# Plain records and interleaved channel pairs in the S4 tables of a fused S4 + MLP training kernel

## The chip, the cores and the metric

The kernel runs on one NeuronCore of a Trainium2 chip. A core has a matrix engine (TensorE, "PE" in the profile, with its weight loads as "PEld"), a vector engine (VectorE, "DVE"), a scalar engine (ScalarE, "ACT"), GpSimd ("POOL") and SyncE ("SP"), which here only starts transfers; 16 DMA engines move the data. The five instruction streams run side by side and meet through semaphores. The metric is the device time of one launch in microseconds.

## What is computed

Sequence length L = 2048, D = 448 channels, N = 256 complex states per channel, MLP width F = 1792, all bf16. The output is a gated sum of a long convolution (the S4 branch `a`) and a two-layer MLP with squared ReLU (`b`); the kernel returns it and 14 gradients.

```python
g  = sigmoid((u * gate_w).sum(-1))
# S4: K[d,l] = Re sum_n C*dt*B*exp(dt*A)^l ; a = irfft(rfft(u) * rfft(K)) + u*Dskip
P  = exp(logdA[:, :, None] * arange(L))
K  = einsum("dn,dnl,dn->dl", Cc, P, dB).real
# MLP
r  = relu(u @ w1 + b1);  b = (r * r) @ w2 + b2
out = g * a + (1 - g) * b
_out, _vjp = jax.vjp(f, A_u, ..., gate_w); grads = _vjp(grad_out)
```

The powers P = lambda^l are never formed for all l. With l = 48 b + s, a table X holds 16 small powers times the weight W = C·dt·B (`Xs`) and a table Y the giant steps (`Ys`); K is the product X·Y, one matmul for each channel and pair of table halves. The gradient of C, B and A needs the transposed sums with dK, the gradient of K.

## The kernel before

**Up to 248 us.** Everything to line 663 is put in order by the compiler's scheduler: loads and a first transform of u and of the gradient (the FFT is done as matmuls; `fwd1`, `fwd2`, `inv1`), and beside them `powers` (L573 to L590): 12 squarings of lambda for four groups of up to four chunks of 32 channels. Each level is copied by ScalarE from float32 into the group's record (L577, into strided fields), squared by ScalarE (L586) and combined by VectorE (L587, L588); the finished records go to DRAM (`rec_d`, L590). The product of the spectra (`cmul`, L274 to L279) and `inv1` end in `hd` in DRAM, which is loaded again (L302); the matmuls of L637 make dK, which goes through DRAM (`dk_d`, L648) back into the tile `DK` (four DMAs, L653 and L654).

**The loop, about 248 to 640 us.** From `tc.manual_schedule()` (L1002) the order of every instruction stream is the order in which the code is written. The loop runs over 14 chunks of 32 channels, and for each chunk over the tokens of one string. The "D" tokens are steps of the MLP (first layer, projection, then the second layer's backward pass), 13 in a chunk, 127 in all:

```python
PERIOD = """XS YS LR D X0 Z0 D SA X1 Z1 D X2 D Z2 D Y0 Y1 SV D T0 Y2 D P0 D S0 Z3 FX0 Y3 D FX1 T1 Y4 KM KO D P1 D FY0 S1 D FY1 FY2 D"""
```

The tokens X, Y, XS, YS, KM and KO work on chunk c, the tokens T, Z, P and S on chunk c-1:

- LR loads the next chunk's record (L718, GpSimd's queue); FX and FY let ScalarE spread it into full-width multipliers (L726 to L737); XS and YS (L713, L741) copy the seeds.
- X0 to X2 double the table X by one product (L683) and one sum (L684) each; Y0 to Y4 do so for Y (L697, L700, sums L706). All VectorE.
- KM (L770) is 128 small TensorE matmuls X·Y into the PSUM tile psX, KO (L777) copies them out, and then starts four DMA transposes of Y (L796, SP's queue), one for each group g of 8 channels.
- SA (four ScalarE copies, L802) and SV (one VectorE product, L806) put dK and 16·b·dK of the chunk into matmul operands `DKc`.
- Z0 to Z3 multiply group g's transposed Y with these (L821, PSUM tile psF) and copy out (ScalarE, L823). T0 and T1 transpose half of X on TensorE, 16 transposes into the same PSUM tile psF (L790). P0 and P1 are two VectorE products of the two (L833, L834), S0 and S1 sum them over 16 entries with a selection matrix (L850).
- A first-layer step is 8 matmuls (L911, L914), two ReLUs on ScalarE (L918) and a square on VectorE two steps later (L921); a second-layer step is 8 matmuls (L973, L976), two scalings (L978) and a VectorE product (L981). A projection half-step is 7 matmuls (L894). The second layer first loads its operand from `DBT_d` in DRAM (L957), which the program starts shortly before.

**Behind the loop.** The last chunk's Z, T, P and S, a reload of K, its transform, another `cmul`, the remaining weight gradients of the MLP as filling work (L1104 to L1123), `param_grads` (L1292 to L1342, a VectorE generator called for four groups of channels) and the outputs.

Of the kernel before, what the change touches and what calls it, by code (L numbers as in the profile page):

```python
# [316 lines left out]
def kernel(ctx, tc, A_u, A_A_re, A_A_im, A_B_re, A_B_im, A_C_re, A_C_im, A_log_dt, A_Dskip,  # L317
# [95 lines left out]
    vw_np = np.array([[slot_offsets().get(i % 64, 0) + 16 * (b if i % 64 < 40 else 0) for b in range(NA)] for i in range(128)], np.float32).astype(ml_dtypes.bfloat16)  # L413
    vw = const.tile([P, NA], bf16, name="vw")
    nc.sync.dma_start(vw[:], nc.inline_tensor(vw_np, name="cs_vw").ap())
# [123 lines left out]
    psets = [(Fp[:, 0:4 * RS], RA[:, 14336:16384], W0[:, 3584:4608]), (RA[:, 0:4 * RS], RA[:, 8704:10752], SB[:, 10240:11264])]  # L539

    def fields(r):

        xs = r[:, :, 0:512].rearrange("p c (t w r e) -> p c t w r e", t=2, r=2, e=2)
        ys = r[:, :, 512:1024].rearrange("p c (w t e) -> p c t w e", t=2, e=4)
        lx = r[:, :, 1024:1408].rearrange("p c (t l w) -> p c t w l", t=2, w=W2)
        ly = r[:, :, 1408:2176].rearrange("p c (t l w) -> p c t w l", t=2, w=W2)
        return xs, ys, lx, ly
    for rb, _, _ in psets:
        xs, ys, _, _ = fields(rb.rearrange("p (c r) -> p c r", c=4))
        for t in range(2):  # L550
            G_.memset(xs[:, :, t, :, 0, 0], 1.0 - t)
            G_.memset(ys[:, :, t, :, 0], 1.0 - t)
            G_.memset(ys[:, :, t, :, 3], 0.0)

# [3 lines left out]
    def powers(gr):  # L558
        nch = min(4, NCH - 4 * gr)
        cs_ = slice(4 * gr, 4 * gr + nch)  # L560
        n = nch * W2
# [11 lines left out]
        S.copy(xs[:, :, :, :, 1, 0], Wt[:, cs_])  # L573
        x, y = Lam[:, :, cs_], halves(cur[0])
        for k in range(NLEV):
            dst = ys[..., 1] if k == 3 else ys[..., 2] if k == 11 else xs[..., 0, 1] if k == 4 else lx[..., LEVX[k]] if k in LEVX else ly[..., LEVY[k]]
            S.copy(dst.rearrange("p c t w -> p t c w"), x)  # L577
# [73 lines left out]
    for cpy in range(2):  # L651
        qe = nc.scalar if cpy else G_
        qe.dma_start(DK[64 * cpy:64 * cpy + 40], bass.AP(tensor=dk_d, offset=0, ap=[[16 * D, 40], [D, 16], [1, D]]))  # L653
        qe.dma_start(DK[64 * cpy + 40:64 * cpy + 41, 0], bass.AP(tensor=dk_d, offset=640 * D, ap=[[D, 1], [1, D]]))  # L654


# [21 lines left out]
    X2 = 2 * W2
    def step_x(c, n, k):

        lo = Xs[c % 2][:, 0:1]
# [1 line left out]
        V.tensor_tensor(out=Vt[:, 0:2 * w * n], in0=run(lo, 0, [0, 2], [NA, w], [1, n]), in1=run(PX[:, 0:1], 512 * k, [2, w], [0, n], [1, 2]), op=ALU.mult)  # L683
# [886 lines left out]
```

## Time and profile before

| | us |
|---|---|
| runs | 915.91, 918.64, 899.32; median 915.91 |
| profiled execution, its span | 902.5 |
| VectorE busy | 635.3 (70%) |
| TensorE busy | 625.3 (69%) |
| ScalarE busy | 512.8 (57%) |
| GpSimd busy | 207.0 (23%) |

The span runs from the first to the last instruction of one profiled execution; its own time outside the profile is not recorded, and the three runs lie between 3 us below the span and 16 us above it. No engine is busy throughout, so the shares over the whole span say little: the program has stages with different limits, and each has to be read by itself. In a row of the trace "x" is a count, "L" a line of the kernel, and the arrow in a wait points to the instruction or transfer that ended it.

### The profile page before, as it was taken

Reading aid. Unit: us, or ns where it says so; the run is one execution under the profiler, and the core shown is the slowest. Engines: PE = TensorE matmul, PEld = TensorE weight load, DVE = VectorE, ACT = ScalarE, POOL = GpSimd, SP = SyncE. Lnnn points to the kernel's source line nnn. Section 1 sums busy time; section 2 is a strip of 40 time slices with the busy share of each in tenths; the row PEclk is TensorE's granted clock in tenths of the full one; section 3 lists DMA queues with packets and bytes.
Section 4 is the critical chain, followed back from the end, with each engine's and each line's share of the span. In section 5 each row is a group of like instructions: output and inputs, shape, how many; then the busy total and the mean of one; then the engine's idle time right before and its main releaser. Section 6 shows DMA issues by size and latency. Waiting matters only on the chain. (4 is left out here: it accounts for less than half of the span.)

```text
span 902.5 us, 16581 instructions
## 1 busy us (share of the span) xinstructions
PE 625.3 (69%) x6596; PEld 301.3 (33%) x6621; DVE 635.3 (70%) x1004; ACT 512.8 (57%) x820; POOL 207.0 (23%) x320
## 2 busy tenths in 40 slices
PE   3755454426178887878667777777779787898794
PEld 1212111102024443435423333343545343444341
DVE  4795997761478889987639877978647865765360
ACT  0777877840366646676544655546566577344451
POOL 1253000141111212211232332313125311131121
PEclk9865555556589999999578997999979899989797
DMA  9858675589387795885696999769769999997951
GB/s 187 220 136 314 241 280 202 197 288 257 88 170 143 164 118 149 174 182 96 105 237 154 193 220 154 219 114 248 179 227 310 357 302 294 297 268 255 221 139 32
DMA packets 183583, 183.40 MB, mean 203 GB/s; under 512 B 124790, under 2 KB 159122, under 8 KB 182914
## 3 DMA queue, kind: packets, MB, share of 16 engines
q1 hardware_dynamic: 151596, 88.98, 44.9%
q0 software_dynamic: 22480, 71.68, 26.9%
q10 hardware_dynamic: 9430, 21.69, 6.8%
q8 instruction: 52, 0.85, 0.4%
q14 instruction: 25, 0.20, 0.1%
HBM read 84.76 MB, written 68.91 MB: 170 GB/s over the span
## 5 line engine op out<-in xcount | busy, mean ns | idle before, releaser
L823 ACT CAST P<-psF 128x1024 bf16<-128x1024 f32 x56 | 62.2, 1112 | 53.8 <-PE psF L821 48.0
L683 DVE TENSOR_TENSOR F<-X,F 128x1024 bf16<-128x1024 bf16 (+2 forms) x42 | 64.3, 1531 | 2.1 <-ACT F L729 1.5
L894 PEld LDWEIGHTS <-U 128*128 128x128 bf16 x448 | 41.9, 102 | 45.9 <-issue 16.3
L911 PE MATMUL psN<-S,K 128*128 128x512 bf16 x155 | 43.8, 414 | 16.3 <-ACT S L918 14.2
L973 PE MATMUL psN<-S,K 128*128 128x512 bf16 x156 | 44.0, 410 | 15.1 <-DMA S<-DBT_d 13.2
L1117 PEld LDWEIGHTS <-S 128*128 128x128 bf16 x416 | 40.0, 101 | 39.7 <-issue 12.0
L1117 PE MATMUL psX<-D,S 128*128 128x449 bf16 x224 | 51.5, 377 | 1.6 <-ACT S L1123 0.7
L833 DVE TENSOR_TENSOR M<-P,psF 128x2048 bf16<-128x2048 bf16 x28 | 34.1, 1217 | 25.2 <-PE psF L790 22.9
L821 PE MATMUL psF<-R,S 41*32 41x256 bf16 x896 | 24.6, 291 | 38.8 <-ACT P L823 22.7
L894 PE MATMUL psN<-D,U 128*128 128x448 bf16 x224 | 51.2, 378 | 0.0
L899 POOL DMA_DIRECT2D br_d<-D x32 | 17.7, 553 | 145.0 <-ACT D L898 142.5
L894 PE MATMUL psN<-S,U 128*128 128x448 bf16 x224 | 50.4, 374 | 0.0
L978 ACT ACTIVATE U<-psN 128x512 bf16<-128x512 f32 x56 | 30.5, 611 | 32.6 <-PE psN L976 32.6
L1108 ACT ACTIVATE S<-psN 128x1024 bf16<-128x1024 bf16 x32 | 33.0, 1030 | 19.4 <-PE psN L1104 19.3
L802 ACT COPY S<-K 128x128 bf16<-128x128 bf16 x56 | 34.9, 1024 | 13.5 <-DMA K<-dk_d 13.5
L1117 PE MATMUL psX<-K,S 128*128 128x448 bf16 x192 | 40.9, 357 | 1.5 <-ACT S L1120 1.5
L790 PE MATMUL psF<-ident,X 128*128 128x128 bf16 x448 | 35.8, 244 | 8.7 <-ACT P L823 8.6
L981 DVE TENSOR_TENSOR U<-U,D 128x1024 bf16<-128x1024 bf16 x28 | 18.9, 688 | 30.1 <-ACT U L978 30.1
L790 PEld LDWEIGHTS <-X 128*128 128x128 bf16 x448 | 32.8, 111 | 15.3 <-issue 13.6
L293 PE MATMUL psN<-D,cb_MI 64*128 64x448 bf16 x48 | 20.4, 553 | 23.6 <-DVE D L276 5.5
L684 DVE TENSOR_TENSOR X<-F 128x512 bf16<-128x512 bf16 (+2 forms) x42 | 35.6, 848 | 1.4
L898 ACT CAST D<-psN 128x448 bf16<-128x448 f32 x32 | 17.2, 536 | 33.4 <-PE psN L894 30.8
(334 smaller groups left out, 1643.9 us busy)
## 6 DMA issues: line engine op xcount, KB each, us to landing
sp<-K ACTq DMA_DIRECT2D x8, 896.0 KB
D<-rT_d POOLq DMA_DIRECT2D x28, 256.0 KB, 6.0
dhT_d<-U POOLq DMA_DIRECT2D x28, 256.0 KB, 4.8
R<-sp SPq DMA_DIRECT2D x8, 896.0 KB
S<-dhT_d POOLq DMA_DIRECT2D x14, 512.0 KB, 5.5
R<-hd SPq DMA_DIRECT2D x16, 448.0 KB
rec<-rec_d POOLq DMA_DIRECT2D x12, 544.0 KB, 7.3
S<-rT_d POOLq DMA_DIRECT2D x12, 512.0 KB, 6.9
```

What stands on the lines that cost most here:

```text
L683: V.tensor_tensor(out=Vt[:, 0:2 * w * n], in0=run(lo, 0, [0, 2], [NA, w], [1, n]), in1=run(PX[:, 0:1], 512 * k, [2, w], [0, n], [1, 2]), o ...
L684: V.tensor_tensor(out=run(lo, n, [NA * X2, 2], [NA, X2], [1, n]), in0=run(vb, 0, [n * X2, 2], [n, X2], [1, n]), in1=run(vb, (w + X2) * n, ...
L790: T_.transpose(ps[:, t, 128 * b:128 * b + 128], Xs[c % 2][:, o_:o_ + 128], ident[:])
L802: S.copy(D2[:, :, 0, 4 * l:4 * l + 4].rearrange("p (g i) a -> p a g i", g=NG), DK[:, l::4].rearrange("p a (e g q i) -> p a e q g i", g=NG, ...
L823: S.copy(zbs[c, g // 2][:, :, g % 2].rearrange("p t h k n -> p t k h n"), psz[:].rearrange("p t (k h n) -> p t k h n", k=2, h=2))
L833: V.tensor_tensor(out=pr.rearrange("p t g h k n -> p t (g h k n)"), in0=zv, in1=xv, op=ALU.mult)
L894: T_.matmul(ps[:, 0:D], lhsT=hblk[:, j, P * tt:P * tt + P], rhs=ws[:, j, :], start=(w == 1 and j == 0), stop=(j == FT - 1))
L911: T_.matmul(pss[k][:], lhsT=w1w[:, dt, j * P:j * P + P], rhs=UT[:, dt, 512 * lb:512 * lb + 512], start=(dt == 0), stop=False, skip_group_c ...
L973: T_.matmul(pss[k][:], lhsT=w2Tw[:, jp, dt, k], rhs=dblk[:, dt], start=(dt == 0), stop=False, skip_group_check=True)
L978: S.mul(hblk[:, 2 * jp + k], pss[k][:], 2.0)
L1108: S.activation(hn(i)[:, 8 * th:8 * th + 8, :], ps[:], ACT.Square if i < FT else ACT.Copy)
L1117: T_.matmul(ps[:, 0:w], lhsT=hn(i)[:, t, :], rhs=(DB2[:, t, :] if i < FT else U[:, t, 0:w]), start=(t == 0), stop=(t == LT - 1))
```

## The change

The tables now hold two channels side by side in the innermost position (an element pair is two channels, not two table entries), and everything around them follows:

- **Records.** 14 plain vectors of 128 numbers a chunk (`RS` 1792 instead of 2176), written in three groups of 4, 7 and 3 chunks with one pair of power buffers in place of two sets. They are loaded by two DMAs: 640 seeds, and nine pieces of 256 bytes a partition straight into a double-buffered multiplier tile `PW`; ScalarE then only makes a copy and a negated copy (`expand`, L735 and L736).
- **X and Y.** Each X product is split in two instructions. The seeds take one copy more, and ones are written once ahead of the loop. The last two levels of Y (`split_y`, L713) are four products without a sum, so Y has 57 columns instead of 41; KO adds the halves (three ScalarE copies, one VectorE sum, L775).
- **dK.** `DK` holds every row twice, in the order of Y's 114 rows, and is loaded by 25 DMAs (L651 and the row behind it) instead of 4. `scale_v` makes both operands by two VectorE products (L802); the ScalarE copies `scale_a` are gone.
- **Z, T, P, S.** A Z is 8 matmuls of 114 rows and 512 columns instead of 16 of 41 rows and 256. T transposes only the half of X that is not multiplied by W: 8 transposes a half, into psX instead of psF. The transposes of Y are of quarters (t, channel half) and no longer of groups, so that Z0 and Z1 need two of them, and Z2 and Z3 all four. `param_grads` multiplies by W itself, six VectorE operations more for each of its four groups.
- **Order.** T1 moves from before KM to behind KO and one D; the square of the first layer is done by ScalarE at once (L915).

The core of the diff:

```diff
-PERIOD = """XS YS LR D X0 Z0 D SA X1 Z1 D X2 D Z2 D Y0 Y1 SV D T0 Y2 D P0 D S0 Z3 FX0 Y3 D FX1 T1 Y4 KM KO D P1 D FY0 S1 D FY1 FY2 D"""
+PERIOD = """XS YS LR D X0 Z0 D X1 Z1 D X2 D Z2 D Y0 Y1 SV D T0 Y2 D P0 D S0 Z3 Y3 D Y4 KM KO D T1 FE D P1 D S1 D"""
 def step_x(c, n, k):
-    V.tensor_tensor(out=Vt[:, 0:2 * w * n], in0=run(lo, 0, [0, 2], [NA, w], [1, n]), in1=run(PX[:, 0:1], 512 * k, [2, w], [0, n], [1, 2]), op=ALU.mult)
+    for r in range(2):
+        V.tensor_tensor(out=run(vb, 128 * n * r, [256 * n, 2], [1, 128 * n]), in0=run(lo, 2048 * r, [0, 2], [32, 64], [1, 2 * n]), in1=factor(c, k, 0, 128, n), op=ALU.mult)
...
+def split_y(c, l, dst, *src):
+    for v in range(2):
+        o_ = run(yb, 2 * dst, [128, 64], [1, 16]) if v == 0 else run(yb, 4096 + 2 * dst + 32, [-4096, 2], [128, 32], [1, 16])
+        V.tensor_tensor(out=o_, in0=run(yb, 0, [128, 64], *src), in1=factor(c, 3 + l, v, 64, 8), op=ALU.mult)
...
+    q.dma_start(PW[c % 2].rearrange("p (l k) -> p l k", k=256)[:, :, 64:192], bass.AP(tensor=rec_d, offset=c * P * RS + 640, ap=[[RS, P], [128, 9], [1, 128]]))
+def expand(c):
+    S.copy(v[:, :, 0], v[:, :, 1])
+    S.mul(v[:, :, 3], v[:, :, 2], -1.0)
 def k_out(c, ps):
-    S.copy(KS[:, :, cp % 4, cc], ps[:].rearrange("p i s -> p s i"))
+    S.copy(ko[:, :, 0:24], ps[:, :, 0:24])
+    S.copy(ko[:, :, 40:41], ps[:, :, 24:25])
+    S.copy(kt, ps[:, :, 41:57])
+    V.tensor_tensor(out=ko[:, :, 24:40], in0=ps[:, :, 25:41], in1=kt, op=ALU.add)
 def scale_v(c):
-    V.tensor_tensor(out=D2[:, :, 1], in0=D2[:, :, 0], in1=run(vw[:, 0:1], 0, [0, CC], [1, NA]), op=ALU.mult)
+    for s_ in range(2):
+        V.tensor_tensor(out=run(DKc[c % 2][:, 0:1], 512 * s_, [2, NA], [32, NA], [1, 2]), in0=dk, in1=run(vw[0:NR, 0:1], 0 if s_ else 2 * NA, [2 if s_ else 0, NA], [0, NA], [1, 2]), op=ALU.mult)
 def back_z(c, g):
+    for s_ in range(2):
+        for k in range(4):
+            T_.matmul(psz[32 * k:32 * k + 32, s_], lhsT=DKc[c % 2][:, 512 * s_ + 128 * g + 32 * k:512 * s_ + 128 * g + 32 * k + 32], rhs=run(YT[0:NR, 0:1], 128 * (8 * g + k), [4096, 2], [512, 2], [1, P]),
...
-                    YTs[c] = [load_yt(c, g) for g in range(NG)]
+                    for j in (0, 2, 1, 3):
+                        load_yt(c, j)
...
+GRP = ((0, 4, Fp), (4, 11, RA), (11, 14, Fp))
-        if q < 2:
-            powers(q + 2)
+        if q == 0:
+            powers(2)
+    for p0, n, r0 in ((0, 24, 0), (50, 16, 24), (82, 16, 24)):
+        for w in range(2):
+            for k in range(4):
+                (nc.scalar if w else nc.sync).dma_start(DK[p0 + w:p0 + 2 * n:2, 4 * k:4 * k + 4], ...)
...
-                later(sq)
+                S.activation(hblk[:, 2 * jp:2 * jp + 2].rearrange("p k l -> p (k l)"), r, ACT.Square)
...
+        mul(x1, Wr, Tr); mul(x2, Wi, Ti); mul(acc, Wr, Ti); sub(WTr, x1, x2)
+        mul(x1, Wi, Tr); stt(nWTi, acc, -1.0, x1, ALU.subtract)
```

Three places show how it moves instructions. First, VectorE at the end of the loop's second chunk, before: the two Y2 products and their sum, P0 (L833, L834; M and P are its tiles), the four products and the sum of Y3 and Y4, P1, and the next chunk's seeds (R and Y are the two Y tables, F the temporary).

```order
L697 TENSOR_TENSOR F_192_1468<-R_188_1460,F_192_1468 128x256x8 x2
L706 TENSOR_TENSOR R_188_1460<-F_192_1468 128x128x16
L833 TENSOR_TENSOR M_193_1469<-P_191_1463,psF_1844 128x2048
L834 TENSOR_TENSOR P_191_1463<-P_191_1463,psF_1844 128x2048
L700 TENSOR_TENSOR F_192_1468<-R_188_1460,F_192_1468 128x128x8 x4
L706 TENSOR_TENSOR R_188_1460<-F_192_1468 128x128x16
L833 TENSOR_TENSOR M_193_1469<-P_191_1463,psF_1924 128x2048
L834 TENSOR_TENSOR P_191_1463<-P_191_1463,psF_1924 128x2048
```

The same place after the change; L828 and L829 are P, L713 is `split_y`, L775 the new sum of KO, which reads the result of KM from psX.

```order
L828 TENSOR_TENSOR M_194_1433<-P_191_1420,psX_1780 128x2048
L829 TENSOR_TENSOR P_191_1420<-P_191_1420,psX_1780 128x2048
L713 TENSOR_TENSOR R_188_1417<-R_188_1417,F_192_1431 128x64x16
L713 TENSOR_TENSOR R_188_1417<-R_188_1417,F_192_1431 128x2x32x16
L713 TENSOR_TENSOR R_188_1417<-R_188_1417,F_192_1431 128x64x16
L713 TENSOR_TENSOR R_188_1417<-R_188_1417,F_192_1431 128x2x32x16
L775 TENSOR_TENSOR P_191_1420<-psX_1843,S_8_163 128x8x16
L828 TENSOR_TENSOR M_194_1433<-P_191_1420,psX_1989 128x2048
L829 TENSOR_TENSOR P_191_1420<-P_191_1420,psX_1989 128x2048
```

The sum of Y4 is gone from VectorE's stream, and between Y4 and P1 stands an instruction that needs KM's result and ScalarE's copy of it. Second, TensorE in the chunk in which the second layer's first step comes (L973 before, L966 after). Before, the end of T1 (L790) and the beginning of KM (L770):

```order
L790 MATMUL psF_4494<-ident,X_190_1462 128x128
L790 LDWEIGHTS X_190_1462
L790 MATMUL psF_4494<-ident,X_190_1462 128x128
L770 LDWEIGHTS X_190_1462
L770 MATMUL psX_4514<-R_188_1460,X_190_1462 32x41
L770 LDWEIGHTS X_190_1462
```

After the change, in the same chunk, the end of the second layer's step that now follows KM directly (L969 is its 64-row part), and T1 (L789):

```order
L969 MATMUL psN_338_4267<-S_8_163,K_180_1253 128x512
L969 LDWEIGHTS K_180_1253
L969 MATMUL psN_339_4268<-S_8_163,K_180_1253 128x512
L789 LDWEIGHTS X_190_1419
L789 MATMUL psX_4279<-ident,X_190_1419 128x128
L789 LDWEIGHTS X_190_1419
```

T1 stood ahead of KM and stands behind KM and a whole D step now, in this chunk behind the step that waits for `DBT_d`; in the others behind a first-layer step, half a projection or a second-layer step. Third, SP's queue of transfers ahead of the loop, after the change (D and P take `hd`, the first K rows the weights w1, the next K rows dK):

```order
L729 DMA rec_1432<-rec_d 128x640
L380 DMA M_178_1242<-c_Ew 128x3712
L311 DMA D_89_656<-hd 64x4x896 x4
L311 DMA P_179_1244<-hd 64x4x896 x4
L730 DMA F_192_1431<-rec_d 128x9x128
L998 DMA K_180_1253<-in_B_w_dram 128x3x1792
L1000 DMA K_180_1253<-in_B_w_dram 64x1792 x2
L651 DMA K_180_1253<-dk_d 24x4x448 x4
L651 DMA K_180_1253<-dk_d 16x4x448 x8
```

Before, SP held no load of dK (two on ScalarE's queue and two on GpSimd's), and the weights w1 stood ahead of the loads of `hd`.

More of the change, by code (lines that the diff above doesn't have):

```diff
@@ L33 @@
 NLEV = 12
-RS = 2176
+RS = 1792
+RC = 2176
 NA = 16
@@ L37 @@
 NY = 41
+NP = 57
 LAG = 2
@@ L412 @@
     make_identity(nc, ident[:])
[L413 to L415 removed]
+    vw_np = np.zeros((P, NA + 1, 2), np.float32)
+    for i in range(2 * NP):
+        p = table_position(i // 2)
+        for b in range(NA):
+            vw_np[i, b, i % 2] = slot_offsets()[p] + 16 * (b if p < 40 else 0)
+        vw_np[i, NA, i % 2] = 1.0
+    vw = const.tile([P, 2 * NA + 2], bf16, name="vw")
+    nc.sync.dma_start(vw[:], nc.inline_tensor(vw_np.reshape(P, -1).astype(ml_dtypes.bfloat16), name="cs_vw").ap())
     dsk_bc = const.tile([P, D], bf16, name="dsk_bc")
@@ L538 @@
     Fp = K.t("F17", [P, 8704])
[L539 to L553, printed above, removed]
+    GRP = ((0, 4, Fp), (4, 11, RA), (11, 14, Fp))
+    cur = [RA[:, 12544 + 1792 * i:14336 + 1792 * i].bitcast(fp32) for i in range(2)]
+    sqr = W0[:, 3584:5376].bitcast(fp32)
     LEVY = {2: 0, 8: 1, 0: 2, 10: 3, 9: 4, 1: 5}
@@ L650, with run @@
                 q.dma_start(bass.AP(tensor=dk_d, offset=128 * e * D, ap=[[D, 16], [16 * D, 8], [1, D]] if e < 5 else [[D, 1], [1, D]]), st_)
[L651 to L654, printed above, removed]
+    for p0, n, r0 in ((0, 24, 0), (50, 16, 24), (82, 16, 24)):
+        for w in range(2):
+            for k in range(4):
+                (nc.scalar if w else nc.sync).dma_start(DK[p0 + w:p0 + 2 * n:2, 4 * k:4 * k + 4], bass.AP(tensor=dk_d, offset=(16 * r0 + k) * D, ap=[[16 * D, n], [4 * D, 4], [1, D]]))
+    nc.scalar.dma_start(DK[48:50, 0], bass.AP(tensor=dk_d, offset=640 * D, ap=[[0, 2], [1, D]]))
+    def run(base, off, *dims):
+        return bass.AP(tensor=base.tensor, offset=base.offset + off, ap=[list(base.ap[0])] + [list(d) for d in dims])
     RB = K.t("R32", [P, 16384])
@@ L678, with factor @@
-    X2 = 2 * W2
+    Pr = [P2[:, 2048 * i:2048 * i + 2048].rearrange("p (s t g n) -> p s t g n", s=2, t=2, g=2) for i in range(2)]
+    vb = Vt[:, 0:1]
+    def factor(c, lv, v, pairs, n):
+        return run(PW[c % 2][:, 0:1], 256 * lv + 128 * v, [2, pairs], [0, n], [1, 2])
     def step_x(c, n, k):
         lo = Xs[c % 2][:, 0:1]
-        w = 2 * X2
-        V.tensor_tensor(out=Vt[:, 0:2 * w * n], in0=run(lo, 0, [0, 2], [NA, w], [1, n]), in1=run(PX[:, 0:1], 512 * k, [2, w], [0, n], [1, 2]), op=ALU.mult)
-        V.tensor_tensor(out=run(lo, n, [NA * X2, 2], [NA, X2], [1, n]), in0=run(vb, 0, [n * X2, 2], [n, X2], [1, n]), in1=run(vb, (w + X2) * n, [-n * X2, 2], [n, X2], [1, n]), op=ALU.add)
@@ L835, in back_p, with back_s @@
+        V.tensor_tensor(out=pr.rearrange("p s t g n -> p s (t g n)"), in0=zv, in1=run(xb, 0, [0, 2], [1, 1024]), op=ALU.mult)
+        V.tensor_tensor(out=z4, in0=z4, in1=run(xb, 512, [0, 2], [-512, 2], [1, 512]), op=ALU.mult)
         return pr, zb
-    def back_s(c, Q, h):
+    def back_s(c, Q, hf):
         nonlocal sps
         cc = c % GC
-        gs = (2 * h, 2 * h + 1)
-        if cc == 0 and h == 0:
+        if cc == 0 and hf == 0:
             sps = K.ps("S", [P, 2, 256])
         for t in range(2):
-            for k in range(2):
-                off = 24 - 16 * cc - 8 * k
-                for gg, g in enumerate(gs):
+            for s_ in range(2):
+                off = 17 - s_ - 16 * cc
+                for gg in range(2):
@@ L1038, in token @@
                 load_rec(c + 1)
-        elif o[0:2] in ("SA", "SV"):
+        elif o == "SV":
             if new:
-                (scale_a if o == "SA" else scale_v)(c)
+                scale_v(c)
         elif o[0] == "X":
```

232 lines of the change are left out of this document (99 added, 133 removed).

## The prediction

> **What bounds the kernel now.** I read the page's first part, then the trace by stages, then the waits of the loop, then one chunk row by row. The page says that no engine is full:
>
> ```profile
> PE 625.3 (69%) x6596; PEld 301.3 (33%) x6621; DVE 635.3 (70%) x1004; ACT 512.8 (57%) x820; POOL 207.0 (23%) x320
> ```
>
> The busy times by stretch (start and end, length, busy of PE, PEld, DVE, ACT, POOL, granted clock, DMA share, GB/s) show where VectorE carries the time:
>
> ```profile
> 187.00:248.10 61.10, 19.18 (x258) 7.59 (x261) 21.56 (x29) 14.87 (x25) 13.92 (x14) 0.58 0.74 205
> 248.10:420.20 172.10, 140.82 (x2015) 69.67 (x2020) 147.09 (x177) 109.80 (x164) 32.66 (x52) 0.92 0.76 148
> 420.20:463.40 43.20, 24.25 (x356) 14.07 (x355) 22.77 (x28) 20.42 (x27) 10.15 (x16) 0.60 0.86 158
> 463.40:640.00 176.60, 134.92 (x1968) 67.75 (x1978) 148.12 (x178) 100.41 (x158) 52.71 (x81) 0.91 0.90 187
> ```
>
> The second row is six chunks beside first-layer steps: 28.7 us each, VectorE 24.5, TensorE 23.5. The fourth is six chunks beside the second layer: 29.4, 24.7, 22.5. So VectorE is idle for only 4.2 and 4.7 us a chunk; its work and its waits together are a chunk's length, and TensorE is 5 to 7 us behind. The third row is the change of layers, a chunk stretched by a wait. The main waits of the loop (who waited, for whom: total, times, longest):
>
> ```profile
> PE psF L821 <- ACT P L823: 21.6, 16, 3.5
> DVE U L981 <- ACT U L978: 26.9, 7, 16.3
> DVE M L833 <- PE psF L790: 19.1, 11, 4.3
> PE psN L973 <- DMA S<-DBT_d: 13.2, 1, 13.2
> PE psF L821 <- DMA R<-R: 10.0, 7, 3.7
> ```
>
> VectorE's own two are P waiting for T (19.1, or 1.5 a chunk) and the second layer's product waiting for ScalarE (26.9, of which 16.3 at the change of layers, so 1.8 a chunk in the second half). TensorE loses 1.7 a chunk to ScalarE's copies of Z and little to the transposes.
>
> **VectorE's work in a chunk.** Durations by form (busy, mean ns):
>
> ```profile
> L706 DVE TENSOR_TENSOR R<-F 128x2048 bf16<-128x2048 bf16 x12 | 14.7, 1225 | 0.4
> L700 DVE TENSOR_TENSOR F<-R,F 128x1024 bf16<-128x1024 bf16 x24 | 15.2, 684 | 0.0
> L683 DVE TENSOR_TENSOR F<-X,F 128x1024 bf16<-128x1024 bf16 x12 | 13.0, 1081 | 0.0
> L683 DVE TENSOR_TENSOR F<-X,F 128x2048 bf16<-128x2048 bf16 x12 | 14.7, 1222 | 0.2
> L806 DVE TENSOR_TENSOR S<-S,vw 128x512 bf16<-128x512 bf16 x12 | 5.0, 419 | 1.2 <-ACT S L802 1.2
> L921 DVE TENSOR_TENSOR U<-S 128x1024 bf16<-128x1024 bf16 x12 | 8.2, 686 | 4.9 <-ACT S L918 4.9
> ```
>
> The Y3/Y4 sum is the 2048-element L706 group (two a chunk, Y2's stays): -1.22. The square leaves VectorE: 28 steps over 6.5 chunks, 4.3 x 0.69 = -2.95 in the first half, nothing in the second. `scale_v` is two products of 512 whose rows are two adjacent elements. The nearest row with such pairs is L683 of 1024 elements: 1081 ns, where the L700 row with longer runs takes 684. Half of 1081, with some fixed part, is 0.62 each, so 1.24 in place of 0.42: +0.82 (from 0, if they cost 0.42 together, to +0.84). X splits each product: two of 1024 cost 1.37 instead of 1.22, but the first gets runs of four where it had two (between 0.42 and 0.63 each, instead of 1.08 together); with a third seed copy I take +0.1 (-0.3 to +0.6). KO's sum of 128 elements is new; half to one of the 419 ns row: +0.3 (0.2 to 0.42). Net: -3.0 a chunk in the first half, 0.0 in the second.
>
> The Trainium skill (VectorE: DVE Perf Modes, What auto-detection actually checks) lets every 16-bit product with a step of one run at two results a cycle, with no condition on the length of a run. By that rule `scale_v` would gain about 0.5 a chunk on my price, 7 us in all. The L683 row of 1024 speaks against it: 1081 ns, nearer the 1222 of twice the elements than the 684 of its equals. By the rule the time would be 901, still within 2%; I give it 0.1 and keep my price.
>
> **The end of a chunk.** One chunk in the second half, TensorE first, then VectorE (start, duration; in brackets the idle before):
>
> ```profile
> 490.18 1.21 PE L790 MATMUL psF<-ident,X 128*128 128x128 bf16 x16
> 491.32 1.32 PE L770 MATMUL psX<-Y,X 128*32 128x41 bf16 x128
> 492.57 1.50 PE L894 MATMUL psN<-S,U 128*128 128x448 bf16 x7
> ```
>
> ```profile
> 488.45 1.22 DVE L706 TENSOR_TENSOR Y<-F 128x2048 bf16<-128x2048 bf16 x1
> 491.50 1.22 DVE L833 TENSOR_TENSOR M<-P,psF 128x2048 bf16<-128x2048 bf16 x1 [1.82 <-PE psF L790]
> ```
>
> Y ends at 489.67, T1 runs beside its end, and P1 starts at 491.50. After the change Y's end releases KM (1.3), then one D (1.5 here, half a projection), then T1 (half of 1.21, 0.6) and only then P1: 3.4, with the semaphores between them 3.7 taken (2.5 if T1 and D overlap with KM's end, 6 if D itself waits). KO's copies and sum lie beside the D step, so they add nothing while that D is there; without it the sum would be next. VectorE has nothing else: the next chunk's X stands behind P1 in its queue. Against 1.5 lost now that is +2.2 a chunk in the first half; in the second a product of the second layer (0.69) fills part, so +1.5. In return T no longer shares psF with Z.
>
> **ScalarE.**
>
> ```profile
> L802 ACT COPY S<-K 128x128 bf16<-128x128 bf16 x48 | 30.0, 1026 | 0.0
> L737 ACT ACTIVATE F<-rec 128x768 bf16<-128x768 bf16 x24 | 19.0, 850 | 0.0
> L734 ACT COPY F<-rec 128x1536 bf16<-128x1536 bf16 x12 | 17.7, 1473 | 0.0
> L729 ACT ACTIVATE F<-rec 128x384 bf16<-128x384 bf16 x24 | 11.3, 523 | 0.0
> L726 ACT COPY F<-rec 128x768 bf16<-128x768 bf16 x12 | 10.0, 836 | 0.0
> L777 ACT CAST P<-psX 128x328 bf16<-128x328 f32 x13 | 5.6, 432 | 20.4 <-PE psX L770 20.4
> L1108 ACT ACTIVATE S<-psN 128x1024 bf16<-128x1024 bf16 x32 | 33.0, 1030 | 19.4 <-PE psN L1104 19.3
> ```
>
> Removed a chunk: the expansion (19.0 + 17.7 + 11.3 + 10.0) / 12 = 4.8 and `scale_a` 30.0 / 12 = 2.5. Added: two of 576 elements, between 523 and 850 each, 1.4 together; two more small copies, +0.4; and in the first half 4.3 squares at 1.03 (a 1024-element ACTIVATE), 4.4. So -1.1 in the first half, -5.5 in the second. ScalarE isn't the bound; what it gives is shorter waits for Z's copies and the L978 scalings behind copies. Of the 1.7 and 1.8 above I take back 0.5 a chunk in the first half and 1.7 in the second (0 to 3), and in the first the 4.9 us that VectorE waited for one tile's ReLUs (0.8 a chunk).
>
> **The transposes.** SP's rows for two chunks, and TensorE in the first of them (Z2, then Z3):
>
> ```profile
> 489.74 12.69 SPq L796 DMA_TRANSPOSE R<-Y  x4
> 515.22 18.26 SPq L796 DMA_TRANSPOSE R<-R  x4
> ```
>
> ```profile
> 502.60 0.41 PE L821 MATMUL psF<-R,S 41*32 41x256 bf16 x16 [1.40 <-ACT P L823]
> 513.52 0.41 PE L821 MATMUL psF<-R,S 41*32 41x256 bf16 x16 [1.97 <-DMA R<-Y]
> ```
>
> Four transposes take 12.7 and 18.3 us only to be issued; Z3 at 513.52 waited for the fourth, which so landed 23.8 us after the start, while Z2 ran at 12.9. Now Z2 needs the fourth as well. Its natural place, counted from the end of Y, is KM 1.3, eight D steps of 1.5 or a little more, T1, S1 and two Z: about 16. Where the fourth lands at 15 nothing happens; at 23.8 TensorE waits 8, and the rest of the chunk behind Z2 (three D, T0, then P0, Y3 and Y4: some 9 us) follows. I take +0.4 a chunk in the first half, where the DMA share is 0.76, and +0.9 in the second, where it is 0.90 (0 to 4). The record's pieces add to this:
>
> ```profile
> q1 hardware_dynamic: 101400, 25.60, 48.7%
> ```
>
> In the 362 us of the loop that I asked for, these small packets took 0.487 x 362 x 16 / 101400 = 0.028 us of one engine each. The 1152 pieces of 256 bytes of a chunk would at that price keep 16 engines busy for 2.0 us; I leave it in the range. A page of the Trainium skill (DMA: Bandwidth & Descriptors, Why small descriptors are slow) gives a 27% overhead for pieces of 256 bytes; no row here has such pieces.
>
> TensorE's own work hardly changes: T halves (-1.2 a chunk), Z has half as many matmuls of twice the columns on half as many array parts (16 take 0.41 now; 0 to +0.4 for each Z), KM has 57 columns for 41 (0 to +0.4). All of that lies in TensorE's slack of 5 us.
>
> **The change of layers.** TensorE and VectorE there:
>
> ```profile
> 458.38 0.58 PE L973 MATMUL psN<-S,K 128*128 128x512 bf16 x1 [13.22 <-DMA S<-DBT_d]
> ```
>
> ```profile
> 462.79 0.69 DVE L981 TENSOR_TENSOR U<-U,D 128x1024 bf16<-128x1024 bf16 x1 [16.28 <-ACT U L978]
> ```
>
> The load decides when the second layer begins. Before, T1 and P1 were over by then; now T1 stands behind the first step, so T1 and P1 (2.45) follow 458 us: +2.5 (0 to +4).
>
> **Ahead of the loop.** ScalarE's cast of the powers, by form and as minimum, median and maximum, and the first `scale_a`:
>
> ```profile
> L577 ACT CAST F<-R 128x512 bf16<-128x512 f32 x22 | 22.5, 1023 | 9.7 <-DVE R L588 9.6
> ```
>
> ```profile
> L577 ACT CAST F<-R x22: 602/619/2531, 77.9 to 166.4; 128x512 bf16<-128x512 f32 x22
> ```
>
> ```profile
> 236.28 2.41 ACT L802 COPY S<-K 128x128 bf16<-128x128 bf16 x4 [13.46 <-DMA K<-dk_d]
> ```
>
> Most casts cost 0.62 and the strided ones up to 2.53; all are plain now, so 22 of them save 22 x (1.02 - 0.62) = 9 us, and the other record buffer's about half as much. ScalarE and VectorE alternate there, and I let 5 of 13 reach the end. Three groups share one pair of buffers, and the third waits until the first has been written to DRAM: from 0 to +6, inside the stretch's other work. The dK load holds the loop's start: VectorE is busy 21.6 of 61.1 us here. Twelve issues on each of two queues replace two on one; behind them goes `scale_a` (-2.4). I take +1.5 together, and -1.5 because `hd` is loaded ahead of the weights. Ahead of the loop: -5 (-12 to +6).
>
> **Behind the loop.**
>
> ```profile
> L1304 DVE TENSOR_TENSOR X<-X,P x16: 404/418/426, 679.0 to 709.5; 128x256 f32<-128x256 f32 x12, 128x256 f32<-128x256 bf16 x4
> ```
>
> ```profile
> 702.50:710.83 8.33, 4.14 (x23) 1.81 (x24) 8.01 (x19) 3.19 (x6) 2.68 (x5) 0.68 1.02 422
> ```
>
> `param_grads` gets six operations of 0.42 for each group. Two groups (12 x 0.42 = 5.0) run between 674 and 711, and at 702.5 VectorE does nothing else until `cmul` begins: +3.5, since part falls into gaps before (0 to 5). Of the two later groups, 0.5 (0 to 2.5). The last chunk's KO is on the path: three copies and a sum for 0.43, +1.
>
> **The sum** (us for one chunk, then in all). First half: -3.0 work, +2.2 P1, -0.8 and -0.5 ScalarE, +0.4 transposes, so -1.7, times 6: -10. Second half: 0.0 + 1.5 - 1.7 + 0.9 = +0.7, times 6: +4. Change of layers +2.5, ahead -5, behind +5. Together -3.5, so a span of 899 against 902.5. The three runs lie -3, +13 and +16 us from that span, +9 in the mean; the changed kernel should then take 908.
>
> **Rivals.** *The waits dissolve (faster).* If the transposes land before Z2 in nearly every chunk, and ScalarE's lighter stream takes the rest of its waits away, the chunks go to VectorE's work plus the 3.7: 25.2 and 27.9 us (21.5 or 24.7, minus 0.5 for the filled product in the second). That is 21 us for the first six and 9 for the second six; with 10 ahead and 7 lost elsewhere -33, and by half of it, which I hold more likely than all, 895. For it: P1's wait is the only new one, and the listed terms take 5.5 us a chunk off ScalarE. Against it: TensorE is busy 23.5 of each chunk and has its own waits.
>
> *Z2 decides (slower).* One mechanism: the fourth transpose lands at 20 or later in most chunks, since the DMA share is already 0.90 and the record's pieces add 2 us. A chunk is then that landing plus the 9 us behind Z2; at 22 it is 31 to 32, 2 to 3 us more than now. Over 12 chunks +30, with the other terms (change of layers +2.5, ahead -5, behind +5) +32 against the span: about 944 as the runs stand. It decides from a landing of 20.5, where the second half stops being even. For it: 23.8 in the quoted chunk, and 18.3 of issue alone in the next. Against it: 12.7 in others.
>
> *It is hidden (same).* VectorE's 3 us of the first half are given back whole to P1's wait and TensorE, the casts ahead were covered by the transforms beside them: 0 to +6, 911 to 918.
>
> **Chances.** A measurement of this kernel can tell about 2% from no change, 18 us: below 898 is faster, above 934 slower. My forecast (the rule's 901 with its 0.1 among it) and the hidden case are both within 2%: 0.34 and 0.16. The waits dissolving has 0.28, all of it faster, with the remaining 0.02 of faster from the front alone. Z2's waits 0.20, slower. Faster 0.30, same 0.50, slower 0.20. The range leaves out the whole of the first rival's -33 and the upper half of the second's cases: 884 to 934; the likeliest case's own is 898 to 920.
>
> **What would show it.** VectorE's rows: L713 four times 0.68 and no sum behind, L802 at 0.62, no L921. Right before L828's P1 an idle of 3 to 4 us put down to L789's T1; under 2 means that this term is too large. TensorE's wait for L815 by a DMA of the transposed Y at Z2: up to 10 us in the chunks with busy DMA. Stretches between the seeds: 27 us in the first half, 30 in the second. Wrong is the forecast if the chunks beside the first layer aren't shorter than 28, if L735 or the record's landing begins to hold X0 of the next chunk, or if the loop starts later than 248 because the 25 loads of dK do.

## The result and the profile after

| | before | after |
|---|---|---|
| median of the runs, us | 912.68 (20 runs, 899.32 to 922.24) | 918.24 (20 runs, 911.03 to 927.73) |
| profiled execution, span, us | 902.5 | 914.5 |

The ratio after to before is 1.0114, with a 95% interval of 1.0076 to 1.0151: slower by about 10 us, less than the 2% that the chances were given for, but clear of noise. The ratio leaves out, as slow, every run over 1.5% above the fastest of its kernel (half of those before, two of those after); over all runs the medians differ by only 5.6 us, or 0.6%. I had forecast a gain of 3.5 us. VectorE and ScalarE did become lighter, as the page's first part shows:

```profile
PE 624.9 (68%) x5929; PEld 285.9 (31%) x5949; DVE 609.5 (67%) x1044; ACT 459.2 (50%) x740; POOL 206.1 (23%) x323
```

VectorE lost 26 us of work and ScalarE 54, and the program got longer. The first seeds of a chunk (L713 before, L720 after) mark where. In both traces, in us:

| stretch | before | after | difference | forecast |
|---|---|---|---|---|
| start of the second chunk | 248.07 | 241.07 | -7.0 | -5 |
| six chunks beside the first layer | 172.1 | 179.6 | +7.5 | -10 |
| change of layers | 43.2 | 44.3 | +1.1 | +2.5 |
| five chunks beside the second layer | 147.8 | 160.6 | +12.8 | +3.5 (0.7 each) |
| last chunk's seeds to the end | 291.4 | 289.0 | -2.4 | +5, and +0.7 for that chunk |

All of the loss is in the loop, and the rest gained 9 us. How the loss divides between the halves of the loop is less sure: in another trace of the same loop (the eighth experiment's, which changes nothing there) the six chunks take 173.9 us, the change of layers 46.9 and the five chunks 159.3. The same stretches after the change, as busy times by stretch (the second row is the six chunks):

```profile
187.00:241.10 54.10, 21.89 (x271) 8.84 (x274) 17.68 (x27) 10.91 (x18) 8.16 (x11) 0.60 0.84 218
241.10:420.70 179.60, 140.31 (x1718) 64.11 (x1725) 128.23 (x182) 109.09 (x156) 39.68 (x59) 0.92 0.72 141
420.70:465.00 44.30, 23.32 (x308) 12.06 (x308) 21.86 (x33) 15.78 (x21) 10.99 (x17) 0.58 0.83 152
465.00:655.00 190.00, 135.19 (x1648) 60.29 (x1655) 142.47 (x208) 73.97 (x123) 58.75 (x86) 0.87 0.77 167
```

In the six chunks VectorE's work fell from 147.1 to 128.2, and its idle time doubled, from 25.0 to 51.4. The waits of the loop say whom it waited for (total, times, longest):

```profile
DVE M L828 <- PE psX L789: 67.1, 19, 19.0
DVE P L775 <- ACT S L774: 43.0, 13, 5.8
PE psF L815 <- DMA R<-Y: 37.0, 7, 9.8
PE psN L966 <- DMA S<-DBT_d: 16.7, 1, 16.7
PE psF L815 <- DMA R<-R: 16.0, 4, 10.1
PE psX L789 <- DVE P L775: 11.3, 10, 3.9
```

P's wait for T was 19.1 and is 67.1, of which 19.0 belongs to the change of layers. The wait of Z's matmuls for the transposes is 53.0; over the whole loop before it was 14.6:

```profile
PE psF L821 <- DMA R<-R: 10.0, 7, 3.7
PE psF L821 <- DMA R<-Y: 4.6, 2, 2.7
```

(The weight loads in front of these matmuls show waits of 22.5 before and 0.8 after; before, most of that is the same time seen a second time.) A chunk beside the first layer shows how the two hang together. SP, TensorE (Z2, then T0), and VectorE (the end of Y2, then P0):

```profile
294.00 15.17 SPq L796 DMA_TRANSPOSE R<-Y  x4
```

```profile
314.43 1.04 PE L815 MATMUL psF<-R,S 114*32 114x512 bf16 x8 [6.26 <-DMA R<-Y]
...
320.31 0.61 PE L789 MATMUL psX<-ident,X 128*128 128x128 bf16 x8
```

```profile
313.54 1.23 DVE L706 TENSOR_TENSOR R<-F 128x2048 bf16<-128x2048 bf16 x1
321.02 1.22 DVE L828 TENSOR_TENSOR M<-P,psX 128x2048 bf16<-128x2048 bf16 x1 [6.25 <-PE psX L789]
```

Z2 was ready 14.2 us after the transposes began (314.43 - 6.26 - 294.00) and waited until 20.4. T0 stands behind it, P0 behind T0, and so the 6.26 us of TensorE came out as 6.25 us of VectorE, which had finished Y2 and had nothing else in its queue. The end of the chunk before that shows the second new wait. VectorE (Y's last products, KO's sum, P1), and ScalarE between:

```profile
291.44 2.50 DVE L713 TENSOR_TENSOR Y<-Y,F 128x1024 bf16<-128x1024 bf16 x4
297.21 0.73 DVE L775 TENSOR_TENSOR P<-psX,S 128x128 bf16<-128x128 f32 x1 [3.28 <-ACT S L774]
298.64 1.22 DVE L828 TENSOR_TENSOR M<-P,psX 128x2048 bf16<-128x2048 bf16 x1 [0.70 <-PE psX L789]
```

```profile
296.05 1.02 ACT L771 CAST P<-psX 128x192 bf16<-128x192 f32 x1
296.56 0.52 ACT L772 CAST P<-psX 128x8 bf16<-128x8 f32 x1
296.59 0.59 ACT L774 COPY S<-psX 128x128 f32<-128x128 f32 x1
```

From the end of Y (293.94) to P1 (298.64) pass 4.7 us; in the six chunks it is 4.1 to 7.6. KO's copies and its sum are in that path, since T1 is written into psX, where KM's result stands until the sum has read it.

### The profile page after: what moved, and what is told of

Its sections match the earlier page's. It is cut to its first block, busy times and chain, and to the rows that moved or that the text cites. A ratio compares the mean times of both kernels' runs of the same rounds, so it can differ in the third digit from the quotient of the medians.

```text
span 914.5 us, 15196 instructions
## 1 busy us (share of the span) xinstructions
PE 624.9 (68%) x5929; PEld 285.9 (31%) x5949; DVE 609.5 (67%) x1044; ACT 459.2 (50%) x740; POOL 206.1 (23%) x323
## 5 line engine op out<-in xcount | busy, mean ns | idle before, releaser
L817 ACT CAST P<-psF 128x1024 bf16<-128x1024 f32 x56 | 56.6, 1011 | 83.3 <-PE psF L815 64.6
L815 PE MATMUL psF<-R,S 114*32 114x512 bf16 x448 | 39.9, 426 | 61.0 <-DMA R<-Y 37.0
L828 DVE TENSOR_TENSOR M<-P,psX 128x2048 bf16<-128x2048 bf16 x28 | 34.1, 1220 | 70.3 <-PE psX L789 67.8
L695 DVE TENSOR_TENSOR F<-X,F 128x512 bf16<-128x512 bf16 (+2 forms) x84 | 61.8, 777 | 5.3 <-ACT F L736 4.3
L906 PE MATMUL psN<-S,K 128*128 128x512 bf16 x158 | 46.4, 428 | 18.1 <-DMA K<-in_B_w_dram 8.7
L966 PE MATMUL psN<-S,K 128*128 128x512 bf16 x158 | 45.2, 415 | 17.7 <-DMA S<-DBT_d 16.7
L889 PE MATMUL psN<-S,U 128*128 128x448 bf16 x224 | 54.1, 391 | 1.1 <-DVE U L974 1.0
L775 DVE TENSOR_TENSOR P<-psX,S 128x128 bf16<-128x128 f32 x14 | 10.2, 729 | 45.5 <-ACT S L774 45.5
L975 POOL DMA_DIRECT2D dhT_d<-U x28 | 20.6, 734 | 64.6 <-DVE U L974 33.6
L829 DVE TENSOR_TENSOR P<-P,psX 128x2048 bf16<-128x2048 bf16 x28 | 34.2, 1220 | 1.0
L1094 DVE COPY S<-psS 128x1024 bf16<-128x1024 bf16 x14 | 9.6, 688 | 35.8 <-PE psS L1092 35.8
```

The source lines that it names most:

```text
L695: V.tensor_tensor(out=run(vb, 128 * n * r, [256 * n, 2], [1, 128 * n]), in0=run(lo, 2048 * r, [0, 2], [32, 64], [1, 2 * n]), in1=factor(c, ...
L815: T_.matmul(psz[32 * k:32 * k + 32, s_], lhsT=DKc[c % 2][:, 512 * s_ + 128 * g + 32 * k:512 * s_ + 128 * g + 32 * k + 32], rhs=run(YT[0:NR ...
L817: S.copy(zbs[c, g // 2][:, :, :, g % 2], psz[:].rearrange("p s (t n) -> p s t n", t=2))
L828: V.tensor_tensor(out=pr.rearrange("p s t g n -> p s (t g n)"), in0=zv, in1=run(xb, 0, [0, 2], [1, 1024]), op=ALU.mult)
L829: V.tensor_tensor(out=z4, in0=z4, in1=run(xb, 512, [0, 2], [-512, 2], [1, 512]), op=ALU.mult)
L889: T_.matmul(ps[:, 0:D], lhsT=hblk[:, j, P * tt:P * tt + P], rhs=ws[:, j, :], start=(w == 1 and j == 0), stop=(j == FT - 1))
```

## The experiments

Three theories. A: Z2 needs the fourth transpose, waits for it, and holds T0 and P0. B: the chain KM, KO, sum, T1, P1 at a chunk's end decides. C: the record's 256-byte pieces slow the transposes. All ratios are to the kernel before, with 95% intervals; the change itself stands at 1.0114 (1.0076 to 1.0151).

**1. Without the need of the third and fourth quarter.**

```diff
-rhs=run(YT[0:NR, 0:1], 128 * (8 * g + k), ...
+rhs=run(YT[0:NR, 0:1], 128 * (8 * (g % 2 if c < NCH - 1 else g) + k), ...
```

> In the loop Z2 and Z3 multiply the first two transposed quarters once more instead of the third and fourth (half of the sums for C, B and A are therefore of the wrong channels; all instructions and transposes stay). Theory A (Z2 waits for the third and fourth transposes, T0 stands behind it on TensorE and P0 behind that on VectorE): VectorE's wait for P0, 23 us over the six chunks beside the first layer, falls below 5, the loop gets 20 to 30 us shorter, the ratio to the kernel before is 0.98 to 0.99. Theory B (the chain KM, KO, sum, T1, P1 at a chunk's end decides): TensorE's wait at Z2 goes too, but chunks stay within 1 us, ratio 1.005 to 1.015. Theory C (the record's 256-byte pieces slow the transposes): as A, since nobody waits for the late ones.

0.969 (0.961 to 0.977). Waits of this kernel over the six chunks beside the first layer:

```profile
DVE P L775 <- ACT S L774: 23.2, 7, 4.3
DVE M L828 <- PE psX L789: 9.5, 9, 2.9
```

P's wait fell from 28.4 to 9.5 there, a chunk takes 26.7 us instead of 29.9, and KO's wait stayed (23.3 before this edit). The direction is A's, and more than A had said. (By the kernel's code Z0 and Z1 read the first two quarters that are issued, and Z2 and Z3 the last two, not all four; it is the last landing that they need.) C isn't told apart here, as its line said.

**2. T0 ahead of Z2.**

```diff
-... X2 D Z2 D Y0 Y1 SV D T0 Y2 D P0 D S0 Z3 ...
+... X2 D T0 D Y0 Y1 SV D Y2 D P0 Z2 D S0 Z3 ...
```

> Only the order changes: T0 stands where Z2 stood, and Z2 behind P0, five D steps later. Same results. Theory A: P0 no longer waits for Z2, and the fourth transpose has some 8 us more; VectorE's wait for P0 falls below 6 us over the six chunks beside the first layer, ratio 0.975 to 0.995. Theory B: P0's wait goes but comes back as a longer wait at the chunk's end, ratio 1.005 to 1.015. Theory C: as A with part of the gain, since transposes later than 25 us still hold Z2.

0.976 (0.966 to 0.986). Waits over the same six chunks:

```profile
DVE P L775 <- ACT S L774: 28.8, 7, 5.9
DVE M L828 <- PE psX L789: 4.9, 6, 1.1
```

The chunks take 26.8 us. This order keeps every instruction of the change and beats both kernels: the change loses by where Z2 stands, not by its arithmetic.

**3. T1 ahead of KM again.** T1 is written into the PSUM tile of Z as before, and P1 stands ahead of KO's sum.

```diff
-        ps = K.ps("X", [P, 2, 4, P], bf16)
+        if hf and c < NCH - 1:
+            ps = K.ps("F", [P, 2, 1024], bf16)[:, 0].rearrange("p (t b x) -> p t b x", t=2, x=P)
+        else:
+            ps = K.ps("X", [P, 2, 4, P], bf16)
-... Y3 D Y4 KM KO D T1 FE D P1 D S1 D
+... Y3 D T1 Y4 KM P1 KO D FE D D S1 D
```

> T1 goes back ahead of KM, into the PSUM tile of Z as before the change, and P1 stands ahead of KO's sum on VectorE; Z2 stays. Same results. Theory B: VectorE's idle at the chunk's end (20 us for KO's sum and 5 for P1 over the six chunks beside the first layer) falls below 10, ratio 0.975 to 0.99. Theory A: the chunk's start comes earlier but the transposes begin at the same place, the time moves into the wait for P0, which grows by 10 us or more over those six chunks; ratio 1.00 to 1.01.

1.0071 (1.0029 to 1.0113), not distinct from the change. In this kernel's waits of the loop (L792 is T, L831 is P) the wait for KO is gone and the one for T0 has grown; of the two T only T0 writes psX here:

```profile
DVE M L831 <- PE psX L792: 54.4, 9, 15.0
...
DVE P L775 <- ACT S L774: 0.7, 2, 0.4
```

P0's waits in the changed kernel's rows add up to 41 us; here they are 54. The growth lies in the five chunks of the second half (17.4 to 28.7), not in the six, where A had put it (23.4 to 25.7). The 43 us of KO's wait were largely not on the path: the transposes start at the end of Y whatever P1 does, and Z2 waits for them. So B is not the limit as long as A is there.

**4. Without the record's small pieces.**

```diff
-        q.dma_start(PW[c % 2]...
+        if c < 2:
+            q.dma_start(PW[c % 2]...
```

> The nine pieces of 256 bytes a partition of the record are loaded for the first two chunks only; the later ones use those multipliers again (wrong powers in 12 chunks). Theory C: the four transposes land 2 us or more earlier, TensorE's wait for them at Z2 (51 us in the loop) falls by half, ratio 0.99 to 1.00. Theories A and B: the pieces come long before the transposes and take little of the DMA engines; wait and ratio stay as they are, 1.005 to 1.015.

1.0054 (1.0009 to 1.0099): its interval overlaps the change's. The waits of Z's matmuls for the transposes are 45.1 in the loop instead of 53.0, far from half, and in the eighth experiment's trace, which has the pieces, they are 49.2. So no effect of C is shown; a part of some 5 us, by the two ratios, is not ruled out.

**5. Both orders at once.** The edits of 2 and 3 together.

> T0 ahead of Z2 and Z2 behind P0 as in the second experiment, and T1 ahead of KM with P1 ahead of KO's sum as in the third. Same results. If the two waits stand one behind the other (theory A, with the chunk's end as the next limit), VectorE's wait at the chunk's end, 60 us in the loop of the second experiment, now falls below 25 and the time falls with it by 10 to 25 us, ratio 0.95 to 0.965. If the transposes' landing or TensorE sets the chunk from here on, the wait only moves: ratio 0.970 to 0.980.

0.978 (0.972 to 0.984), no better than the second alone: the wait only moved. VectorE's wait for KO's sum fell from 60.4 us in the loop to 3.5, and P's wait for T1 on psF is 40.1. T1 ahead of KM needs Z3's copy out of psF first (6.9 us in the loop), KM stands behind T1, and with KM all that follows it.

**6. The kernel before with the new order of T0 and Z2.** The same edit of the token string as in 2, in the kernel before.

> The kernel before with the same new order of T0 and Z2. There Z2 needs three transposes and T0 shares the PSUM tile psF with Z, so Z2 must wait for P0's read. If the gain of the second experiment is one of order alone, this kernel gains as much, ratio 0.97 to 0.985. If it comes from the lighter chunk that the change made possible, with T in another PSUM tile, this gains nothing or loses: ratio 0.995 to 1.03.

1.019 (1.014 to 1.025). The waits of this kernel (L834 is P's second product) name the reason:

```profile
PEld L821 <- DVE P L834: 42.3, 11, 6.7
PE psF L821 <- DVE P L834: 38.7, 10, 6.3
```

T and Z share psF there, so Z2 waits for P0's read of T. In the old kernel, then, this order does not pay. That T in psX, which the change brought, is what lets it pay was not tried by itself.

**7. The second experiment with the square on VectorE.**

```diff
-                S.activation(hblk[...], r, ACT.Square)
+                def sq(jp=jp, r=r):
+                    V.tensor_tensor(out=hblk[...], in0=r, in1=r, op=ALU.mult)
+                later(sq)
```

> The second experiment with the first layer's square back on VectorE, two steps late. If VectorE's work counts once the wait for P0 is gone, the six chunks beside the first layer get 2 to 3 us longer each, and the ratio rises from 0.976 to 0.99 to 0.995. If the chunk's end or TensorE decides there, the squares fall into idle time and the ratio stays within 0.972 to 0.982.

1.0008 (0.996 to 1.0056). The six chunks take 29.4 us each (243.65 to 420.20) instead of 26.8: 2.6 more, of 4.3 x 0.69 = 3.0 moved, and the ratio rises a little further than the line said. With the wait for Z2 gone, VectorE's work counts almost one to one. In the change as made it did not: 19 us less work there, and longer chunks.

**8. Without the new products of `param_grads`.** The two lines with `Tr` and `Ti` are taken out.

> The changed kernel without the six new products of param_grads (the gradients of A lack the factor W). The prediction priced them at 4 us behind the loop: ratio 1.005 to 1.008 instead of 1.011, and the stretch from the last chunk's seeds to the end 4 us shorter than 289. If TensorE's filling work and the DMAs set that stretch, it stays within 287 to 293 and the ratio at 1.009 to 1.014.

1.0155 (1.007 to 1.024); from the last chunk's seeds to the end it takes 910.0 - 620.8 = 289.2 us, against 289.0 with the products. No gain is seen, so they are probably hidden; but the interval still reaches the 1.005 to 1.008 of the priced case, and that stretch differs by more than 4 us between the traces here, so it is not shown.

**9. The kernel before, with the fourth transpose needed by Z2.**

```diff
-                    YTs[c] = [load_yt(c, g) for g in range(NG)]
+                    ys_ = {g: load_yt(c, g) for g in (0, 1, 3, 2)}
+                    YTs[c] = [ys_[g] for g in range(NG)]
```

> The kernel before, with one edit: the four transposes of a chunk are issued in the order 0, 1, 3, 2, so that Z2 needs the last of them as it does after the change, and Z3 needs nothing more. Same results, same instructions. Theory A: this dependence costs the kernel before too; it has P0 behind the same T0 and Z2, so TensorE's wait for the transposes grows from 23 us in the loop to 40 or more and the ratio is 1.005 to 1.025. If the dependence only bites because the changed chunk's other work became shorter, the wait moves from Z3 to Z2 and the ratio stays within 0.997 to 1.004.

1.056 (1.050 to 1.063), more than twice what A said. Nothing but the order of two transposes differs, and the kernel before loses some 51 us to it. In its traced run (970.9 us) the waits of Z's matmuls for the transposes are 92.2 us instead of 14.6, and P's wait for T, which was 19.1, is 69.8:

```profile
DVE M L833 <- PE psF L790: 69.8, 12, 16.0
PE psF L821 <- DMA R<-Y: 52.2, 7, 17.2
PE psF L821 <- DMA R<-R: 40.0, 8, 11.3
```

Why the old kernel loses so much more to it than the change does was not taken apart; its chunks carry more work, which is a likely reason. This is the part of the change that costs, put into the old kernel by itself.

**10. Z2 and Z3 later still.**

```diff
-... D P0 Z2 D S0 Z3 Y3 D Y4 KM ...
+... D P0 D S0 Z2 Y3 D Z3 Y4 KM ...
```

> The second experiment with Z2 behind S0 and Z3 one D later, directly ahead of Y4's last products and KM. Same results. If the remaining waits for transposes in the second half (27 us in the loop, the longest 12.6) are what holds the second experiment, they fall below 12 and the ratio from 0.976 to 0.96 to 0.97. If the next limit is the chunk's end, the wait moves there (Z3's copy then holds P1, and the next transposes start later): 0.972 to 0.985.

0.980 (0.972 to 0.988). The waits of Z's matmuls for the transposes are 5.3 in the loop, the wait for KO's sum is 60.7: the second case. No gain is seen from moving Z2 past the second experiment's place.

**11 and 12. T1 directly behind KM.** The fifth experiment with `Y4 KM T1 P1 KO` in place of `T1 Y4 KM P1 KO`, and the same with Z2 and Z3 where the tenth has them.

> As the fifth experiment (T0 ahead of Z2, Z2 behind P0, T1 in Z's PSUM tile, P1 ahead of KO's sum), but T1 directly behind KM instead of ahead of it, so that KM doesn't wait for Z3's copy. Same results. If that wait (7 us for T1 in the loop, and the shift of KM) held the fifth experiment, VectorE's wait for P falls below 35 from 49 and the ratio from 0.978 to 0.965 to 0.972. If the transposes set the chunk, 0.972 to 0.985.

> The tenth experiment (Z2 behind S0, Z3 ahead of Y4's last products) with T1 in Z's PSUM tile directly behind KM and P1 ahead of KO's sum. Same results. The waits for transposes stay below 10 us in the loop, as in the tenth, and the wait at the chunk's end, 61 us there, falls to about 2 a chunk: ratio 0.96 to 0.97. If Z3's copy then holds T1 and P1, the ratio stays within 0.972 to 0.985.

0.965 (0.955 to 0.974) and 0.973 (0.966 to 0.981). The eleventh, with a median of 879.9 us, is the fastest version here. Its waits in the loop:

```profile
DVE M L831 <- PE psF L792: 39.7, 12, 9.8
...
PE psF L818 <- DMA R<-Y: 15.1, 4, 11.2
...
PE psF L818 <- DMA R<-R: 10.6, 6, 4.4
```

P's wait is 44 with the 4.7 us on psX, not below 35 as its line had it. The intervals of 5, 11 and 12 touch, so that T1's better place is likely, and not shown, to be what the eleventh gains over the fifth. In the twelfth the wait for KO's sum is 3.0, but P still waits some 60 us in all, for T and for ScalarE. The ratio is that of its second case, though Z3's copy, named there as the reason, held T1 for only 2.1 us.

## Why the prediction was wrong

**The step that failed** is the term of the transposes: "I take +0.4 a chunk in the first half, where the DMA share is 0.76, and +0.9 in the second". Z2 waited 7.5, 1.5, 6.3, 0, 3.4 and 0 us for its transposes in the six chunks, 18.6 or 3.1 a chunk, and 22.8 in the five, 4.6 a chunk. P0, behind it, waited 8.4, 0.3, 6.3, 1.8, 4.1 and 2.7 us in the six chunks, 23.4 or 3.9 a chunk, and 17.4 in the five, 3.5 a chunk; in the fourth and sixth chunk Z2 did not wait, so those 4.5 us have another cause. Together with 23.3 at KO's sum and 5.0 at P1 this is nearly all of VectorE's 51.4 us of idle time in the six chunks. The mechanism had been named, and as the second rival; its size was off. The +0.4 and +0.9 were chosen, not added up from landings chunk by chunk. Z2's natural place was put at about 16 us behind Y's end; in the nine chunks of the loop in which it waited, it was ready 12.3 to 16.9 us after the transposes began, 15.0 in the mean, and the last of them landed after 17.4 to 27.0. A chunk whose transposes land late pays, and one whose transposes land early gets nothing back. The ninth experiment gives the price in the old kernel, 1.056; the first and the second, from the other side, 1.0114 to 0.969 and 0.976.

**Which rival came true.** "Z2 decides", in its place and its mechanism, not in its size: +30 over the loop was said, and the loop lost 20 (7.5 + 12.8), and its own price is larger than that, since VectorE's lighter work was gained beside it. It was given 0.20. That 918 us lies within the stated 884 to 934, and at the edge of what "It is hidden" gave (911 to 918), is luck: it is a sum of errors of both signs, with 18.9 us of VectorE's work saved in the first half alone and more than that lost to two new waits.

**VectorE's work** was right: -18 forecast for the six chunks, -18.9 measured, with these forms after the change:

```profile
L802 DVE TENSOR_TENSOR S<-K,vw 114x512 bf16<-114x512 bf16 x26 | 13.1, 582 | 0.0
L695 DVE TENSOR_TENSOR F<-X,F 128x512 bf16<-128x512 bf16 x24 | 9.1, 422 | 0.0
L775 DVE TENSOR_TENSOR P<-psX,S 128x128 bf16<-128x128 f32 x12 | 8.7, 728 | 40.0 <-ACT S L774 40.0
```

`scale_v` cost 1.16 (1.24 taken), so the row with pairs was the better guide. KO's sum cost 0.73 where 0.3 was taken. By the rule in the Trainium skill (VectorE: DVE Perf Modes, What auto-detection actually checks), `scale_v`'s products would have been near the 422 ns of L695's runs of four. The trace does not agree: they took 582. (From the prediction's rows that rule would have gained 0.4 us a chunk, not the 0.5 that it gives.)

**The chunk's end** was priced at 3.7 us from Y to P1, and measures 4.9 in the mean of the six chunks. The sentence that KO's copies and sum "lie beside the D step, so they add nothing" was wrong: T1 waits for the sum because both use psX (11.3 us in the loop), and the copies are slow:

```profile
L771 ACT CAST P<-psX 128x192 bf16<-128x192 f32 x12 | 12.2, 1014 | 13.2 <-PE psX L763 13.1
L774 ACT COPY S<-psX 128x128 f32<-128x128 f32 x12 | 6.9, 578 | 0.0
L772 ACT CAST P<-psX 128x8 bf16<-128x8 f32 x12 | 6.1, 507 | 0.0
```

One copy of 328 elements had cost 432 ns. These three overlap in time and take 1.13 us together (296.05 to 297.18 in the chunk shown), where "+0.4" had been added to the 0.43. For the change's time this hardly mattered, by the third experiment. That it matters once the order is mended is likely from the eleventh, but not shown: its interval overlaps the second's.

**ScalarE.** The expansion and `scale_a` went as said, but ScalarE's busy time in the six chunks stayed at 109 (109.8 before) instead of falling by 6.6. KO's copies explain some 2 us of that; the rest was not taken apart. The waits that the relief was to shorten did shrink: VectorE's for the second layer's scalings from 10.6 us outside the change of layers to 3.6, and TensorE's for Z's copies from 21.6 to 7.3. The chunks did not get shorter by the 1.7 us that this was to bring in the second half, since other waits ended last; it was not tried by itself.

**The change of layers** cost +1.1 for +2.5, with P1 behind the waiting step as foreseen (19.0 of P's wait).

**Ahead of the loop** the sign and about the size were right, -7.0 for -5, but as a sum of two larger parts. VectorE's first cast of dK comes 14.1 us earlier than before the change (217.11 before), and the first `scale_v` 8.0 earlier (238.72 before):

```profile
203.03 0.62 DVE L236 CAST st<-psN 128x448 bf16<-128x448 f32 x1 [18.11 <-PE psN L634]
207.73 0.62 DVE L236 CAST st<-psN 128x448 bf16<-128x448 f32 x1 [4.08 <-PE psN L634]
212.66 0.76 DVE L695 TENSOR_TENSOR F<-X,F 128x512 bf16<-128x512 bf16 x2 [4.31 <-ACT F L736]
213.51 0.61 DVE L236 CAST st<-psF 1x448 bf16<-1x448 f32 x1
...
230.72 1.03 DVE L802 TENSOR_TENSOR S<-K,vw 114x512 bf16<-114x512 bf16 x2 [8.50 <-DMA K<-dk_d]
```

Between them lie the other casts of dK and its load, whose twelve issues alone take SP 10.6 us. The first row is ScalarE's copy of the multipliers, with its own casts of dK behind it:

```profile
211.38 0.67 ACT L735 COPY F<-F 128x576 bf16<-128x576 bf16 x1 [4.09 <-DMA F<-rec_d]
218.14 10.63 SPq L651 DMA_DIRECT2D K<-dk_d  x12
```

The load begins 15.1 us after the first cast (9.9 before, 226.99 - 217.11), because the last casts stand behind work that waits for the record's multipliers; from there to `scale_v` it takes 12.6 us (11.7 before). So powers and spectra gained about 14, the record's late landing gave 5 back, and the load with `scale_a` gone 0.9, where 1.5 had been taken. That "the record's landing begins to hold X0" had been named as a sign of being wrong; it came here, ahead of the loop. The parts were not tried by themselves.

**Behind the loop** the +5 was not there. By the eighth experiment `param_grads` is probably hidden, though its work stands in VectorE's queue; the -2.4 itself lies within the 9 us (285.6 to 294.9) by which that stretch differs between the traces of the changed kernel and its variants here.

## What to carry to other kernels

When a new layout makes a step need the last of several transfers instead of an earlier one, look at what stands behind that step in its engine's queue: the wait is paid by all of it, chunk by chunk. Price such a wait from each chunk's own landing, not from the mean. Then move the waiting step behind work that does not need it: here two tokens moved in an order string turned 1.011 into 0.976, and with the end of the chunk reordered too 0.965.
